# State reads of an attention stage: four matmuls of 32 by 64 on column tiles in place of one of 128 by 256

## The chip, the cores and the metric

The kernel runs on one core of a Trainium2 chip. A time is that of one execution on the device, in microseconds (us), from the first to the last instruction and what the launch puts around it. Shorter is better. The engines of the core are named as in the profile: PE is TensorE's matmuls and PEld its weight loads, DVE is VectorE, ACT is ScalarE, POOL is GpSimd, SP is the queue of SyncE, which here only issues DMAs.

## The reference

Three layers follow each other: an attention between 512 tokens and 32 state vectors for each of 8 batches and 8 heads, a top-1 mixture of experts with a capacity, and a gated feed-forward layer.

```python
B, H, S, Ns, D = (8, 8, 512, 32, 64)
scores = scale * np.matmul(x, state.transpose(0, 1, 3, 2))
a = softmax(scores); xread = np.matmul(a, state)
scores2 = scale * np.matmul(state, x.transpose(0, 1, 3, 2))
a2 = softmax(scores2)
sread = np.matmul(a2, x)                       # the state reads: 32 x 512 by 512 x 64, per batch and head
x = np.concatenate([xread, sread], axis=2)     # then gate, greedy assignment, experts, feed-forward
```

## The kernel before

The kernel is one program for one core. Its attention stage takes the batches b = 0 to 7 in turn. A string of steps for each batch (HEAD, ORDER, NEXT, LAST, TAIL, lines 53 to 57) says in which order the code is written; a scheduler under it then sets each engine's order from dependences and a cost table of its own, so a step can end up beside one of the next batch. The steps that matter here:

- z (`scores`, L302 to L304): scores of four heads at a time (g = 0, 1), state index by head on the 128 partitions (head h of the group on partitions 32h to 32h+31), the 512 tokens on the free axis.
- f (`exps2`, L324 to L326): row maximum on DVE, exponential `e2` on ACT. t (`turn_e2`, L350, L351): PE turns `e2` so that tokens lie on partitions; ACT copies the result to `et`.
- m (`center`, L310 to L314) and e (`exps1`, L335 to L338): the other softmax, DVE `zt`, POOL `zc`, DVE `zb`, ACT `e1h` and `zb`, POOL `e1l`. r (`xread`, L357 to L383): the token reads `px` from these, copied by ACT (`xu`, L374).
- s (`sread`, L414 to L439): the state reads. For each g the four token blocks r add up in `ps`. The weights are the 128 columns of `et` (four heads by 32 states), and the moving side holds the 256 columns of the four heads (4 by 64). So all 4 by 4 pairs of heads are computed and the four diagonal blocks are used. DVE then multiplies each diagonal block by `rd2` into `ss` (L433, four instructions of 32 partitions by 128), SP stores `ss` to `xm_d` in four DMAs (L438).
- G (`sread_gate`, L441 to L451): PE turns `ss` (L443), ACT copies it to `TS` (L444), and after the fourth and the eighth batch PE multiplies `TS` by the gate's weights (L449).
- p (`prep_state`, L241 to L254: ACT `SBh` L247, DVE `SBl` L252, ACT `sT` L254), q (`prep_gate`, L262 to L270: PE with 64 rows of weights, ACT `SC` and `RBh`, POOL `RBl`), x (`turn_x`, L285 to L289): operands of the next batch.

A float32 matmul of the program stands in the trace as two pairs of weight load and matmul: the 64 matmuls of L422 are 128 there. The last steps of the stage (TAIL) go over into the selection: `keys` and `count128` (L506, L517) need the gate's results of the last batch. The selection, the experts and the feed-forward layer follow; they are the other 1240 us of the program.

Of the kernel before, what the change touches and what calls it, by code (L numbers as in the profile page):

```python
# [21 lines left out]
F32 = mybir.dt.float32  # L22
# [9 lines left out]
B, H, S, D, NS = 8, 8, 512, 64, 32  # L32
# [32 lines left out]
def moe_kernel(ctx: ExitStack, tc: tile.TileContext, x, state, moe_w_gate, moe_w1, moe_w2,  # L65
               moe2_w_gate, moe2_w_val, moe2_w_out, out):
    nc = tc.nc
# [25 lines left out]
    ap = a_ctx.enter_context(tc.tile_pool(name="ap", bufs=1, space=PSUM))  # L93
# [38 lines left out]
    for q in range(2):  # L132
        pair = []
        for part in "hl":
            t = ac.tile([128, 4, 128], FR, name=f"SB{part}{q}")
# [3 lines left out]
    for q in range(3):  # L139
        pair = []  # L140
        for part in "hl":
            t = ac.tile([128, 2, 4, ROW], FR, name=f"RB{part}{q}")
# [271 lines left out]
    def sread(b, part):  # L414
        t = st[b]
        xc, et = xcs[b], t["et"]
        if part == 0:
            t["ps"] = ap.tile([128, 2, 256], F32, name="ps")
        ps = t["ps"]
        for g in (part,):  # L420
            for r in range(4):
                nc.tensor.matmul(ps[:, g, :], et[:, r, g, :],  # L422
                                 xc[:, r, 4 * g:4 * g + 4, :].rearrange("p h d -> p (h d)"),
                                 start=(r == 0), stop=(r == 3))
        if part == 0:
            return
        rd2 = aw.tile([128, 2], F32, name="rd2")
        nc.vector.tensor_scalar(rd2, t["den2"], 1e-9, None, op0=OP.add)
        nc.vector.reciprocal(rd2, rd2)
        ss = aw.tile([128, 2, D], F32, name="ss")  # L430
        for h in range(4):
            p = slice(32 * h, 32 * h + 32)
            nc.vector.tensor_mul(ss[p], ps[p, :, 64 * h:64 * h + 64],  # L433
                                 rd2[p, :, None].to_broadcast([32, 2, D]))
        r0 = b * SE + S
        for h in range(4):
            dst = xm_d[r0:r0 + NS].rearrange("n (g h d) -> n g h d", g=2, h=4)[:, :, h, :]
            nc.sync.dma_start(dst, ss[32 * h:32 * h + 32])  # L438
        t["ss"] = ss  # L439
# [266 lines left out]
    for b in range(B + 1):  # L706
        steps = {0: HEAD, B - 2: NEXT, B - 1: LAST, B: TAIL}.get(b, ORDER)
        for op in steps.split():
# [5 lines left out]
            elif k == "m" and b < B:  # L714
                center(b, q)
            elif k == "f" and b < B:
                exps2(b, q)
            elif k == "e" and b < B:
                exps1(b, q)
            elif k == "q" and b + 1 < B:  # L720
                prep_gate(b + 1)
            elif k == "R":
                read_gate(b - 1)
            elif k == "r":
                xread(b - 1, q)
            elif k == "t":
                turn_e2(b - 1, q)
            elif k == "x" and b + 1 < B:
                turn_x(b + 1, q)
            elif k == "s":  # L730
                sread(b - 1, q)
            elif k == "g":
                sread_gate(b - 1)
            elif k == "G" and b > 1:
                sread_gate(b - 2)
            elif k == "p" and b + 1 < B:
                prep_state(b + 1)
            elif k == "k":
                keys(0, PRE, True)
                part_p = ap.tile([128, 512], F32, name="pt", bufs=3)  # L740
                count128(0, PRE, part_p[:, :E])
                part = sel.tile([128, E], F32, name="part")
                nc.vector.tensor_copy(part, part_p[:, :E])
# [664 lines left out]
    for s, (gi, jj) in enumerate(outs):  # L1408
# [5 lines left out]
        if s + 1 < len(outs):  # L1414
            r, t = SETS[s % 2] if s > 1 else YR
# [82 lines left out]
```

## Time and profile before

| | us |
|---|---|
| median of 3 runs (1386.87 to 1389.83) | 1388.23 |
| the profiled execution | 1388.9 |
| its span, first to last instruction | 1387.1 |
| PE busy in the span | 1338.2 |
| PE at L422 (state reads), 128 matmuls, busy | 31.1 |
| DVE at L433 (`ss`), 32 instructions, busy | 9.1 |

Busy time of PE is the union of matmuls whose ends are modelled, and each such matmul lies over the start of the next; so what a matmul costs in a row of them is read from the start of one to the start of the next. "Idle before" is what an engine waited, with the engine that ended the wait.

### The profile page before, as it was taken

What the parts mean: (1) busy time and instruction counts of PE and PEld (TensorE: products, weight loads), DVE (VectorE), ACT (ScalarE), POOL (GpSimd) and SP (SyncE); (2) the same over time, 40 slices, a digit from 0 to 9 for tenths busy, and PEclk for the clock granted to TensorE, in tenths of its full rate; (3) what the DMA queues carried; (4) which work ended last, traced back from release to release, by engine and by line L of the source; (5) the groups of instructions that cost most, each with busy time, mean ns of one, the idle gap of its engine ahead of it and who ended that gap; (6) DMA issues with size and microseconds to landing.
All of it is one profiled execution on the core that took longest, in us unless ns stands there. A gap on an engine that the chain in (4) does not pass through costs nothing.

```text
span 1387.1 us, 27011 instructions
## 1 busy us (share of the span) xinstructions
PE 1338.2 (96%) x10176; PEld 1301.4 (94%) x10177; DVE 1068.7 (77%) x2211; ACT 572.3 (41%) x1175; POOL 440.1 (32%) x378
## 2 busy tenths in 40 slices
PE   6998599999999999999999999999999999999997
PEld 4887489999999999999999999999999999999997
DVE  6878788886887664668777787878777678888784
ACT  5886334233333343434233343434343354344342
POOL 6666111110101010343223120111111008788883
PEclk9999699999999999999999999999999999999999
DMA  7551325544445454536654676787665584444432
GB/s 138 125 128 69 135 83 183 184 157 144 160 159 161 157 176 149 188 109 245 209 199 149 216 245 207 253 259 240 219 221 174 192 279 131 144 152 143 163 108 77
DMA packets 151251, 236.89 MB, mean 171 GB/s; under 512 B 57808, under 2 KB 77264, under 8 KB 150096
## 3 DMA queue, kind: packets, MB, share of 16 engines
q1 hardware_dynamic: 138016, 208.38, 46.1%
q0 software_dynamic: 5536, 17.83, 3.9%
q10 hardware_dynamic: 7568, 8.95, 2.1%
q8 instruction: 80, 1.31, 0.4%
q14 instruction: 51, 0.42, 0.1%
HBM read 151.22 MB, written 83.89 MB: 170 GB/s over the span
## 4 chain that ended last, share of the span: by engine, by line
PE 50%; DMA 1%; DVE 1%; POOL 0%; issue 0%; POOLq 0%; SPq 0%; DVEq 0%
PE b L1157 50%; DMA mt_d<-m 1%; DMA raw<-v_d 0%; DMA v_d<-f32v 0%; POOL tt L930 0%; DVE yb L887 0%; POOL tt L929 0%; DVE m L1203 0%; POOL tt L928 0%; POOL tt L927 0%; POOLq L1493 0%; DVE u L1215 0%; DVE f32v L233 0%; DVE f32v L231 0%; DVE m L1222 0%
## 5 line engine op out<-in xcount | busy, mean ns | idle before, releaser
L1157 PE MATMUL b<-yb,w 128*128 128x364 f32 (+1 forms) x3024 | 500.5, 328 | 2.9 <-DVE m L1203 2.9
L1157 PEld LDWEIGHTS b<-yb,w 128*128 128x128 f32 x3024 | 499.5, 188 | 3.8 <-DVE m L1203 3.8
L1157 PE MATMUL b<-w,yb 128*128 128x256 f32 x2160 | 256.0, 281 | 0.0
L1157 PEld LDWEIGHTS b<-w,yb 128*128 128x128 f32 x2160 | 255.6, 189 | 0.3 <-issue 0.2
L846 PE MATMUL h<-xh,w 128*128 128x288 f32 (+1 forms) x1024 | 207.9, 295 | 1.5 <-ACT xh L830 1.2
L846 PEld LDWEIGHTS h<-xh,w 128*128 128x128 f32 x1024 | 161.6, 189 | 2.5 <-ACT xh L830 1.8
L816 POOL DMA_INDIRECT xg<-xm_d,idx x38 | 45.7, 1203 | 360.3 <-PE bt L825 155.7
L846 PE MATMUL h<-xl,w 128*128 128x288 f32 (+1 forms) x512 | 147.9, 291 | 0.0
L861 PE MATMUL y<-hh,w 128*128 128x288 f32 (+1 forms) x512 | 136.1, 292 | 0.1
L862 PE MATMUL y<-hh,w 128*128 128x288 f32 (+1 forms) x512 | 135.8, 291 | 0.0
L850 ACT ACTIVATE hh<-h 128x288 fp32r<-128x288 f32 (+1 forms) x128 | 50.8, 397 | 186.5 <-PE h L846 173.3
L1204 ACT ACTIVATE m<-m 128x364 f32<-128x364 f32 (+1 forms) x108 | 54.8, 507 | 156.0 <-DVE m L1203 147.7
L887 DVE TENSOR_TENSOR yb<-ty,yb 128x512 fp32r<-128x512 f32 (+2 forms) x96 | 87.8, 921 | 18.8 <-ACT yb L886 17.0
L861 PEld LDWEIGHTS y<-hh,w 128*128 128x128 f32 x512 | 96.6, 189 | 0.3 <-ACT hh L850 0.3
L862 PEld LDWEIGHTS y<-hh,w 128*128 128x128 f32 x512 | 96.7, 189 | 0.0
L846 PEld LDWEIGHTS h<-xl,w 128*128 128x128 f32 x512 | 96.1, 189 | 0.3 <-DVE xl L831 0.2
L914 POOL TENSOR_TENSOR tt<-raw 128x512 f32<-128x512 f32 (+1 forms) x23 | 29.6, 1290 | 208.3 <-DMA raw<-m_d 154.4
L851 DVE SCALAR_TENSOR_TENSOR hl<-h,hh 128x288 fp32r<-128x288 f32 (+1 forms) x128 | 56.0, 438 | 51.4 <-ACT hh L850 50.8
L886 ACT CAST yb<-ty 128x512 fp32r<-128x512 f32 (+2 forms) x96 | 66.5, 694 | 68.9 <-POOL ty L915 33.9
L865 PE MATMUL y<-hl,w 128*128 128x288 f32 (+1 forms) x512 | 87.9, 291 | 0.0
L887 DVE TENSOR_TENSOR yb<-yr,yb 128x512 fp32r<-128x512 f32 (+2 forms) x73 | 71.6, 982 | 6.3 <-ACT yb L886 5.5
L1207 DVE TENSOR_TENSOR m<-cv,m 128x364 f32<-128x364 f32 (+1 forms) x108 | 66.1, 612 | 9.4
(284 smaller groups left out, 2230.5 us busy)
## 6 DMA issues: line engine op xcount, KB each, us to landing
raw<-in_moe_w_dram SPq DMA_DIRECT2D x64, 512.0 KB, 4.8
raw<-m_d SPq DMA_DIRECT2D x14, 1024.0 KB, 5.6
raw<-v_d SPq DMA_DIRECT2D x26, 512.0 KB, 4.5
yr<-m_d SPq DMA_DIRECT2D x13, 1024.0 KB, 5.2
yr<-y_d SPq DMA_DIRECT2D x7, 1456.0 KB, 7.7
v_d<-f32v SPq DMA_DIRECT2D x36, 256.0 KB, 3.5
m_d<-m SPq DMA_DIRECT2D x48, 182.0 KB, 3.0
m_d<-m SPq DMA_DIRECT2D x24, 364.0 KB, 4.5
```

Of the source, the lines that this page charges most:

```text
L816: hooks["g"] = nc.gpsimd.indirect_dma_start(out=xg[:n], out_offset=None, in_=xm_d, in_offset=bass.IndirectOffsetOnAxis(ap=idx[i][:n, j:j + ...
L846: hooks["p"] = nc.tensor.matmul(ph, W[i][0][k][q == 1][:, fs], (xl if q == 2 else xh)[:, k, :T], start=(n == 0), stop=(n == 11)).ins
L850: relu[16 * i + 8 * hf + f] = hooks["hh"] = nc.scalar.activation(hh, ph, AF.Relu).ins
L851: lower[16 * i + 8 * hf + f] = hooks["h"] = nc.vector.scalar_tensor_tensor(hl, ph, 0.0, f32(hh), op0=OP.max, op1=OP.subtract).ins
L861: nc.tensor.matmul(p[d], wh[:, f % 2, ds_], hh, start=(f == 0), stop=False)
L862: nc.tensor.matmul(p[d], wl[:, f % 2, ds_], hh, start=False, stop=False)
L865: nc.tensor.matmul(p[d], wh[:, f % 2, ds_], hl, start=False, stop=(f == 7))
L886: nc.scalar.copy(hi, src)
L887: nc.vector.tensor_tensor(lo, src, f32(hi), OP.subtract)
L1157: nc.tensor.matmul(out, a, b, skip_group_check=True, start=start and n == 0, stop=stop and n == len(terms) - 1)
L1204: hooks["silu"] = nc.scalar.activation(m[:, l], m[:, l], AF.Silu).ins
L1207: hooks["gate"] = nc.vector.tensor_tensor(m[:, l], c, m[:, l], OP.mult).ins
```

## The change

Each matmul of `sread` becomes four. Head h of the group gets a matmul of its own with the 32 weight columns that belong to it, the 64 moving columns that belong to it, and the output partitions 32h to 32h+31, which puts it on column tile h of the array (all 128 rows, 32 columns). Only the diagonal blocks are computed. `ps` shrinks from 256 to 64 columns for each g, and since the blocks of the four heads then stand under each other, one multiplication of 128 partitions by 128 replaces the four of 32. Each half g of a batch has 16 matmuls in the program (32 pairs of load and matmul) where it had 4 (8 pairs); over the stage 64 become 256, and 32 instructions of DVE become 8. The four stores of `ss` stay.

```diff
-            t["ps"] = ap.tile([128, 2, 256], F32, name="ps")
+            t["ps"] = ap.tile([128, 2, D], F32, name="ps")
...
             for r in range(4):
-                nc.tensor.matmul(ps[:, g, :], et[:, r, g, :],
-                                 xc[:, r, 4 * g:4 * g + 4, :].rearrange("p h d -> p (h d)"),
-                                 start=(r == 0), stop=(r == 3))
+                for h in range(4):
+                    p = slice(32 * h, 32 * h + 32)
+                    nc.tensor.matmul(ps[p, g, :], et[:, r, g, p], xc[:, r, 4 * g + h, :],
+                                     start=(r == 0), stop=(r == 3))
...
         ss = aw.tile([128, 2, D], F32, name="ss")
-        for h in range(4):
-            p = slice(32 * h, 32 * h + 32)
-            nc.vector.tensor_mul(ss[p], ps[p, :, 64 * h:64 * h + 64],
-                                 rd2[p, :, None].to_broadcast([32, 2, D]))
+        nc.vector.tensor_mul(ss, ps, rd2[:, :, None].to_broadcast([128, 2, D]))
```

The scheduler's order changes with it, from the first state read on and up to the last matmuls of the attention stage; the order of everything behind is the same. Three places of a batch in the middle of the stage show it.

DVE, from the fourth-to-last `SBl` (low part of the next batch's state) to `zb` (the turned scores that ACT waits for), before:

```order
L252 TENSOR_TENSOR SBl_101<-pt,SBh_99 64x2x32
L380 TENSOR_TENSOR xw<-xu,rd 128x128
L382 COPY rm<-rd 128x16
L252 TENSOR_TENSOR SBl_101<-pt,SBh_99 64x2x32
L387 TENSOR_REDUCE Lw<-xw 128x32
L252 TENSOR_TENSOR SBl_101<-pt,SBh_99 64x2x32
L310 STREAM_TRANSPOSE zt<-z_611 128x512
L324 TENSOR_REDUCE mx<-z_650 128x1
L312 TENSOR_REDUCE m_667<-zt 128x16
L325 TENSOR_SCALAR nmx<-mx 128x1
L289 TENSOR_TENSOR xTl<-pt,xTh 128x4x128 x2
L310 STREAM_TRANSPOSE zt<-z_650 128x512
```

and now:

```order
L382 COPY rm<-rd 128x16
L387 TENSOR_REDUCE Lw<-xw 128x32
L310 STREAM_TRANSPOSE zt<-z_632 128x512
L252 TENSOR_TENSOR SBl_101<-pt,SBh_99 64x2x32 x4
L312 TENSOR_REDUCE m_688<-zt 128x16
L324 TENSOR_REDUCE mx<-z_671 128x1
L289 TENSOR_TENSOR xTl<-pt,xTh 128x4x128
L325 TENSOR_SCALAR nmx<-mx 128x1
L289 TENSOR_TENSOR xTl<-pt,xTh 128x4x128
L335 STREAM_TRANSPOSE zb<-zc 128x512
```

`xw`, `rm`, `Lw` and the first `zt` moved ahead of the four `SBl`, and `zb` follows the second `xTl` directly; the second `zt` comes behind it.

ACT in the same batch, from the second `zb` to the copy `TS` of the state reads, before:

```order
L337 ACTIVATE zb<-zb 128x512
L266 COPY SC<-pt 32x2x8 x4
L269 CAST RBh_103<-SC 32x2x74 x4
L374 COPY xu<-px 128x296 x2
L247 CAST SBh_95<-pt 64x2x32 x4
L351 COPY et<-pt 128x512 x2
L326 ACTIVATE e_827,den_826<-z_819,nmx 128x512
L254 COPY sT<-pt 64x256
L444 COPY TS<-pt 128x4x32
```

and now:

```order
L266 COPY SC<-pt 32x2x8 x4
L269 CAST RBh_103<-SC 32x2x74 x4
L374 COPY xu<-px 128x296
L336 ACTIVATE e1h<-zb 128x512
L374 COPY xu<-px 128x296
L337 ACTIVATE zb<-zb 128x512
L247 CAST SBh_95<-pt 64x2x32 x2
L326 ACTIVATE e_869,den_868<-z_861,nmx 128x512
L247 CAST SBh_95<-pt 64x2x32 x2
L351 COPY et<-pt 128x512 x2
L442 COPY TS<-pt 128x4x32
```

The second `e1h` and `zb` moved behind `RBh`, and `TS` follows `et` directly, where `e` and `sT` stood between the two.

PE in the one batch of the middle that has the gate's matmuls on `TS` (L449 before, L447 now), before:

```order
L443 MATMUL pt<-ident,ss 128x128
L357 MATMUL px<-RBh_107,e1h 128x296
L358 MATMUL px<-RBl_109,e1h 128x296
L359 MATMUL px<-RBh_107,e1l 128x296
L449 MATMUL pt<-wgp,TS 128x8 x4
L285 MATMUL pt<-ident,xc 128x128 x4
```

and now:

```order
L441 MATMUL pt<-ident,ss 128x128
L359 MATMUL px<-RBh_107,e1l 128x296
L357 MATMUL px<-RBh_107,e1h 128x296
L358 MATMUL px<-RBl_109,e1h 128x296
L359 MATMUL px<-RBh_107,e1l 128x296
L447 MATMUL pt<-wgp,TS 128x8 x4
L285 MATMUL pt<-ident,xc 128x128 x4
```

Four token reads stand between the turn of `ss` and the gate's matmuls, where three stood.

## Rows read from the trace of the kernel before

**Rows 1.** Window of the attention's middle: length, busy by engine (instructions), granted clock, DMA
```profile
34.03:116.56 82.53, 79.34 (x472) 68.21 (x470) 69.16 (x182) 71.21 (x203) 57.00 (x58) 0.98 0.47 119
```
**Rows 2.** Windows by batch, between first score matmuls; engines PE, PEld, DVE, ACT, POOL
```profile
70.09:84.37 14.28, 13.88 (x86) 11.80 (x85) 12.33 (x34) 12.67 (x37) 10.23 (x12) 1.00 0.64 155
84.37:102.16 17.79, 16.20 (x94) 14.03 (x92) 13.47 (x37) 13.25 (x40) 11.26 (x11) 0.90 0.51 122
```
**Rows 3.** Timeline of PE, one batch: start, length, instruction, count
```profile
75.11 0.38 PE L357 MATMUL px<-RBh,e1h 128*128 128x296 f32 x1
...
76.84 1.89 PE L422 MATMUL ps<-xc,et 128*128 128x256 f32 x8
...
78.70 0.30 PE L358 MATMUL px<-RBl,e1h 128*128 128x296 f32 x1
...
81.06 1.89 PE L422 MATMUL ps<-xc,et 128*128 128x256 f32 x8
82.88 0.63 PE L262 MATMUL pt<-wg,sT 64*128 64x32 f32 x4
83.44 0.40 PE L357 MATMUL px<-RBh,e1h 128*128 128x296 f32 x1
```
**Rows 4.** Timeline of weight loads at L262 of another batch: idle before, and its end
```profile
68.61 0.52 PEld L262 LDWEIGHTS pt<-wg,sT 64*128 64x128 f32 x4 [0.33 <-issue]
```
**Rows 5.** Line L517: lengths in ns, first and last start
```profile
L517 PE MATMUL pt<-G,I x24: 165/167/181, 138.7 to 139.3; 128*128 128x8 bf16 x24
```
**Rows 6.** Timelines of ACT and POOL in that batch: start, length, idle before
```profile
69.99 0.71 ACT L266 COPY SC<-pt 32x16 f32<-32x16 f32 x4
...
72.68 0.87 ACT L247 CAST SBh<-pt 64x64 fp32r<-64x64 f32 x4
...
74.67 0.69 ACT L326 ACTIVATE e<-z,nmx 128x512 f32<-128x512 f32 x1
...
80.44 0.63 ACT L336 ACTIVATE e1h<-zb 128x512 fp32r<-128x512 f32 x1 [0.46 <-DVE zb L335]
...
83.03 0.66 ACT L336 ACTIVATE e1h<-zb 128x512 fp32r<-128x512 f32 x1
...
84.26 0.72 ACT L266 COPY SC<-pt 32x16 f32<-32x16 f32 x4
...
84.33 1.28 POOL L338 TENSOR_TENSOR e1l<-zb,e1h 128x512 fp32r<-128x512 f32 x1
```
**Rows 7.** Timeline of DVE in that batch, and one row of the stage's end
```profile
75.66 0.23 DVE L252 TENSOR_TENSOR SBl<-pt,SBh 64x64 fp32r<-64x64 f32 x1
...
76.56 0.65 DVE L324 TENSOR_REDUCE mx<-z 128x1 f32<-128x512 f32 x1
77.25 0.69 DVE L312 TENSOR_REDUCE m<-zt 128x16 f32<-128x512 f32 x1
...
77.91 1.28 DVE L289 TENSOR_TENSOR xTl<-pt,xTh 128x512 fp32r<-128x512 f32 x2
...
79.73 0.67 DVE L335 STREAM_TRANSPOSE zb<-zc 128x512 f32<-128x512 f32 x1
...
84.05 1.22 DVE L433 TENSOR_TENSOR ss<-ps,rd 32x128 f32<-32x128 f32 x4
...
119.42 0.29 DVE L380 TENSOR_TENSOR xw<-xu,rd 128x128 f32<-128x128 f32 x1
```
**Rows 8.** PE at the gate's matmuls, and the window right behind, columns as in Rows 1
```profile
90.75 1.06 PE L449 MATMUL pt<-wgp,TS 128*128 128x8 f32 x8 [1.52 <-ACT TS L444]
91.66 0.73 PE L285 MATMUL pt<-ident,xc 128*128 128x128 f32 x4
...
92.06:95.48 3.42, 3.42 (x14) 3.06 (x12) 2.25 (x5) 2.26 (x5) 1.05 (x1) 0.50 1.08 307
```
**Rows 9.** Timelines of PE and DVE at the end of the attention stage
```profile
132.83 3.70 PE L422 MATMUL ps<-xc,et 128*128 128x256 f32 x16
...
146.69 0.17 DVE L530 TENSOR_TENSOR ev<-acc,part 128x8 f32<-128x8 f32 x1 [1.02 <-PE acc L517]
```

## The prediction

> **What bounds the kernel now.** I read the windows first, to see where the changed lines run, then the timelines of one batch engine by engine, to see who waits for whom. The state reads run in the attention stage only; its middle, 82.53 us, holds five and a half rounds of one batch each [rows 1]. No engine is alone the bound there. In a round of 14.28 us PE is busy 13.88, ACT 12.67, DVE 12.33 and POOL 10.23 [rows 2], and PE's share is flattered, because each of its matmuls is drawn over the start of the next. The reader should look for the loop that sets the 14.28. It is this: ACT begins `e1h` when DVE's `zb` is done (80.44, after 0.46 idle), works on to `SC` at 84.26 and to the end of `SBh`, which in the round before came at 73.55, 3.56 after the `SC` at 69.99 [rows 6]; DVE then goes from its first `SBl` to the end of `zb` at 80.40 [rows 7], and ACT begins again. That is 3.82 + 3.56 + 6.85, or 14.2. Neither the state reads on PE nor the products `ss` on DVE lie on this loop. So the change gains in the middle only by way of what the new order does to the loop, or loses if PE becomes longer than it.
>
> **A second loop goes over PE.** `SC` starts, ACT comes to the second `zb`, POOL makes `e1l`, PE does the token reads, both blocks of state reads and L262, and the next `SC` may start. Before, it has some slack. In the new order the second `e1h` and `zb` come behind `RBh`. From `SC` to the end of that `zb` are 3.56 less 0.87 for `SBh` plus 1.23 for the two (83.03 to 84.26), or 3.9; `e1l` adds 1.28 [rows 6]. On PE, 1.7 pass from the first token read to the first block, 2.5 between the end of that block (78.56, which is the start of L358 less the 0.14 of a token read) and the second, and 0.66 for L262 with what stands before it [rows 3]. That makes 10.1 without the two blocks.
>
> **The blocks.** Removed: 8 pairs of load and matmul at 0.215 (76.84 to 78.56) in each block, 3.44 a round [rows 3]. Added: 64 pairs a round, each with a quarter of the weight columns and a quarter of the moving columns. The trace has no column tile, so the price of a pair is bounded. One matmul of 64 columns streams a quarter of 0.215, 54 ns. The cheapest pair in the trace is 26 ns: 24 pairs with 8 moving columns start within 0.6 us [rows 5]; four tiles that work side by side can come down to it. The dearest would add a load that hides under nothing: L262 has four pairs in 0.56 with loads of 128 columns, 0.14 each [rows 3], 27 ns for 32 columns in proportion, so 81 ns a pair; 0.19 if a load of 32 columns costs as much as one of 128. I take 40 ns. The two pairs of one float32 matmul go to the same tile, so each second pair must wait 54 ns for its own tile, and each other one needs the 26 of the cheapest row; it is nearest to the row of L517. The block's own loads before hide wholly under the running matmul, since 0.215 is the streaming time alone.
>
> The trace does show what another shape of weights costs. Before L262, with 64 rows, the weight load has 0.33 idle that no engine ended [rows 4]. The block's last matmul stops streaming at 82.78, and L262 starts at 82.88 [rows 3], 0.1 later, and its first load is not hidden. I take 0.12 to enter a block (0.1 and a load of 27 ns) and 0.2 to leave it (0.1 and a load of 128 columns). The second block already runs into L262, so only three of the four passages are new: 0.44 a round.
>
> At 40 ns PE's loop is thus 10.1 + 2.6 + 0.4, or 13.1. At 26 ns it is 12.2, at 54 ns 14.0, at 81 ns 15.7.
>
> [...]
>
> **ACT and DVE in the new order.** ACT's part from `e1h` to the end of `SBh`: 3.82 + 3.56 as before, and `e`, 0.69, which now stands between the `SBh`: 8.1 [rows 6]. DVE's part is now four `SBl` (0.9), `m` 0.69, `mx` 0.65, `xTl` 1.28 and `zb` 0.67, 4.2 [rows 7]; `xw`, `Lw` and both `zt` moved out of it. With 0.3 for the small steps and hand-overs this loop is 12.6, which is ACT's whole work in a round [rows 2]. The products `ss` fall from 1.22 to the 0.29 of the nearest product of 128 by 128 [rows 7], 0.9 less on DVE, whose sum becomes 11.4; that alone ends nothing sooner. If it cost nothing less, DVE would still fit. So PE's 13.1 is late next. The real round is longer than its longest loop, as engines meet on buffers, and I take 13.3: **1.0 less a round**, 5.0 over five rounds (no gain counted in the half one).
>
> **The gate's matmuls.** One round takes 17.79 [rows 2]. [...] In the new order ACT copies `TS` directly behind `et`, not behind `e` and `sT`, and PE has one token read more to do first. The excess of 3.51 less the 0.9 that stays is 2.6; I take 2.3, and 1.5 if the clock falls all the same.
>
> **The end.** In the last batch PE works on 16 matmuls of state reads from 132.83 on, 3.4 at 0.215, and at the end DVE waits 1.02 for PE [rows 9]. 64 pairs at 40 ns and the passages save 0.6 there; four products less in `ss` save 0.9, of which part waits behind PE's queue. I take 1.2 less for both. The stores of `ss` stay four on SP, and each now waits for the one product, which is over sooner than the fourth was; SP's other DMAs, the loads of `xc`, keep their distance.
>
> Behind the attention stage the order is the same and starts sooner by as much. **Sum** against the profiled execution's 1388.9: less 5.0, 2.3 and 1.2, which is 8.5: 1380.4. That execution is 0.7 above the median of the runs, so their spread adds no more than that.
>
> **The rivals.** *One tile after the other.* The array streams the four tiles in turn and hides the loads: 54 ns a pair, PE's loop 14.0, only 0.3 less a round. With 2.3 at the gate and 0.5 at the end that is 4.3 less, 1384.6. The change would then not do what it says. For it: every row of the trace shows one matmul after the other; against it: no row has two tiles.
>
> *Loads in the open.* The pair costs 81 ns: PE's loop of 15.7 becomes the bound of every round, 1.4 more each, 7.0; the end costs 1.3 more and the gate gains 1.5, so 6.8 more: 1395.7, slower. From 58 ns a pair PE's loop is longer than today's round; from about 66 ns the total is a loss. Against it: the loads of L422 hide today; for it: those of L262 don't at its start. At 0.19 the kernel would be at some 1430, to which I give next to nothing.
> [...]
>
> *A slower clock.* PE has less to stream and idles more; if the clock falls once a round as at 92.06, each fall costs the 1.1 that remain of the 3.51 beside the wait and L449. Five and the one at the gate take 6.6 of the 8.5: 1387.0. For it: the fall followed 1.5 of idle time; against it: the rounds beside it have 0.4 idle and a clock of 1.00 [rows 2].
>
> **How the numbers follow.** About 0.2% (2.8 us) is what a measurement of this kernel can tell from no change. My forecast has 0.50: 0.45 faster, 0.03 within, 0.02 slower, as the new order can also lose. One tile after the other 0.20: 0.13, 0.05, 0.02. Loads in the open 0.18: 0, 0.02, 0.16. Slower clock 0.12: 0.04, 0.05, 0.03. Together faster 0.62, within 0.15, slower 0.23. The range 1374 to 1391 goes from a pair of 26 ns with rounds near ACT's 12.7 (1.6 less each, 5.0 + 3.0 + 3.5) to the slower clock and one tile after the other with the order losing some; it leaves out most of the loads in the open and little below, under 0.2.
>
> **What would show it.** Right: blocks of 32 pairs in 1.2 to 1.4 us on PE, rounds of 13 to 13.5, no wait for `TS` over 0.3, a clock of 1.00 up to the stage's end, `ss` in one instruction of about 0.3. Wrong: blocks of 1.8 (one tile after the other) or over 2.5 (loads in the open), rounds of 14 or more, falls of the clock inside rounds, or a round set by POOL, which has no part in the sum.

## The result

| | before | after |
|---|---|---|
| median, us | 1388.49 (1386.87 to 1389.83) | 1375.22 (1374.47 to 1376.23) |
| the profiled execution | 1388.9 | 1376.23 |
| its span | 1387.1 | 1374.5 |

After to before is 0.9905, 95% interval [0.9888, 0.9923]: faster by 13.3 us, where 8.5 was forecast. The span is 12.5 shorter (1387.05 and 1374.53 before rounding). In the lines below, line numbers of after are those of before less 2 from `ss` on, and 2 more in `sread`'s matmul: L424 (before L422), L432 (L433), L441 (L443), L447 (L449).

A round below goes from a batch's first score matmul to the next batch's; the gate's round is the one that holds the gate's matmuls on `TS`, and the three full rounds ahead of it are called plain. The windows by batch of the kernel after, with columns as in [rows 2] (length, busy time of PE, PEld, DVE, ACT, POOL with counts, granted clock, DMA share and rate): a plain round, the gate's round and the last round.

```profile
65.74:78.61 12.87, 11.79 (x131) 10.01 (x131) 12.08 (x31) 12.24 (x37) 10.26 (x11) 1.00 0.74 170
78.61:92.54 13.93, 12.94 (x139) 11.00 (x139) 12.35 (x32) 12.53 (x37) 10.29 (x11) 1.00 0.75 172
92.54:107.19 14.65, 12.76 (x136) 10.45 (x135) 12.55 (x31) 14.09 (x45) 12.94 (x16) 1.00 0.35 107
```

A plain round takes 12.87 where it took 14.28, the gate's 13.93 where it took 17.79 [rows 2], both at a clock of 1.00. PE's busy time in a plain round is 2.1 shorter. ACT, with 12.24 of 12.87, is now the fullest engine, with DVE right behind it. The only wait of ACT that the view of this plain round names is short:

```profile
ACT e L326 <- DVE nmx L325: 0.3, 1, 0.3
```

So the round is now little more than ACT's own work.

The timeline of PE after, over the first block of a round, its waits in the next round, and at the gate's matmuls. The first three rows are the same block, cut off after one, four and eight pairs:

```profile
61.03 0.24 PE L424 MATMUL ps<-xc,et 128*32 128x64 f32 x1
61.03 0.26 PE L424 MATMUL ps<-xc,et 128*32 128x64 f32 x4
61.03 0.32 PE L424 MATMUL ps<-xc,et 128*32 128x64 f32 x8
61.03 0.65 PE L424 MATMUL ps<-xc,et 128*32 128x64 f32 x32
61.61 0.41 PE L357 MATMUL px<-RBh,e1h 128*128 128x296 f32 x1
...
67.89 0.50 PE L303 MATMUL z<-xTl,SBh 128*128 128x512 f32 x1 [0.72 <-DVE xTl L289]
...
72.24 0.33 PE L441 MATMUL pt<-ident,ss 128*128 128x128 f32 x1 [0.26 <-ACT et L351]
...
85.70 0.31 PE L359 MATMUL px<-RBh,e1l 128*128 128x296 f32 x1
85.85 1.02 PE L447 MATMUL pt<-wgp,TS 128*128 128x8 f32 x8
```

Four pairs start within 0.02 us (0.26 less the 0.24 that the first is drawn). The next four come 0.08 later, and each further four 0.056 after those before. The trace does not name the tile of a pair; with 54 ns of streaming a pair [rows 3], four starts every 56 ns read as one on each column tile. The 32 pairs start within 0.43 (0.65 less the 0.22 that a later one is drawn), 14 ns a pair, and the next instruction starts 0.58 after the block's start; a block took 1.72 before [rows 3]. PE now waits 0.72 for DVE's `xTl` and 0.26 for ACT's `et` in a round, and not at all for `TS`.

Timelines of POOL and DVE after, in a plain round and at the stage's end:

```profile
65.88 1.34 POOL L338 TENSOR_TENSOR e1l<-zb,e1h 128x512 fp32r<-128x512 f32 x1
...
65.99 1.26 DVE L382 COPY rm<-rd 128x16 f32<-128x16 f32 x1
...
67.76 0.27 DVE L432 TENSOR_TENSOR ss<-ps,rd 128x128 f32<-128x128 f32 x1
...
70.81 0.16 DVE L382 COPY rm<-rd 128x16 f32<-128x16 f32 x1
...
118.73 1.96 POOL L383 TENSOR_TENSOR xm<-xu,rm 128x1024 f32<-128x1024 f32 x1 [2.23 <-ACT zb L337]
...
118.91 1.81 DVE L478 TENSOR_TENSOR key<-V,sg 128x24 int32<-128x24 int32 x1
...
134.85 0.17 DVE L528 TENSOR_TENSOR ev<-acc,part 128x8 f32<-128x8 f32 x1 [0.17 <-PE acc L515]
```

`ss` is one product of 0.27. The last row stood at 146.69 before [rows 9], so the attention stage gives 11.84 of the span's 12.5. One copy `rm`, 128 by 16, takes 0.16, and another of the same size 1.26, beside an `e1l` of POOL that began 0.1 before it; `key`, a small operation too, takes 1.81 and ends with an `xm`. The prediction has no term for these rows.

In the five rounds of the stage's middle the clock is 1.00, but not up to the stage's end. Windows there, before and then after:

```profile
139.00:147.00 8.00, 7.65 (x64) 7.47 (x61) 4.91 (x27) 4.69 (x24) 0.00 (x0) 0.57 0.29 110
```

```profile
124.00:135.00 11.00, 10.81 (x122) 10.45 (x123) 7.53 (x35) 5.00 (x25) 1.91 (x1) 0.53 0.27 104
```

In the last stretch of the stage the granted clock of the changed kernel is at 0.50 for some 10 us (a mean of 0.53 over these 11.00) where that of the kernel before was for some 7 (0.57 over 8.00). Ahead of the first full round it is the other way round: a mean clock of 0.81 over 18.12 us before, 0.89 over 16.03 after.

### The profile page after: what moved, and what is told of

Read it like the earlier page. It is cut to its first block, busy times and chain, and to the rows that moved or that the text cites. A ratio compares the mean times of both kernels' runs of the same rounds, so it can differ in the third digit from the quotient of the medians.

```text
span 1374.5 us, 27733 instructions
## 1 busy us (share of the span) xinstructions
PE 1322.4 (96%) x10560; PEld 1286.9 (94%) x10561; DVE 1067.5 (78%) x2187; ACT 568.9 (41%) x1175; POOL 439.7 (32%) x378
## 4 chain that ended last, share of the span: by engine, by line
PE 51%; DMA 1%; DVE 1%; issue 0%; ACT 0%; POOLq 0%; DVEq 0%; SPq 0%
PE b L1155 51%; DMA yr<-m_d 1%; ACT yb L884 0%; DVE m L1201 0%; DVE yb L885 0%; DVE m L1205 0%; ACT m L1202 0%; DMA mt_d<-m 0%; DVE u L1213 0%; POOLq L1491 0%; DVE w L885 0%; ACT w L884 0%; DVE cv L1204 0%; DVE m L1220 0%; DVEq L1201 0%
## 5 line engine op out<-in xcount | busy, mean ns | idle before, releaser
L885 DVE TENSOR_TENSOR yb<-ty,yb 128x512 fp32r<-128x512 f32 (+2 forms) x96 | 88.0, 924 | 18.2 <-ACT yb L884 17.1
L1205 DVE TENSOR_TENSOR m<-cv,m 128x364 f32<-128x364 f32 (+1 forms) x108 | 69.1, 640 | 10.2 <-ACT m L1202 1.1
```

Source lines behind the costliest of these rows:

```text
L885: nc.vector.tensor_tensor(lo, src, f32(hi), OP.subtract)
L1205: hooks["gate"] = nc.vector.tensor_tensor(m[:, l], c, m[:, l], OP.mult).ins
```

## The experiments

**How the order was separated from the instructions.** The scheduler gave the changed kernel another order, so the change is three things at once: blocks, products and order. In most of the kernels below every instruction of the attention stage is chained behind the one that goes ahead of it on its engine, in an order read off one of the two kernels ("old order", "new order"). This fixes the issue order and is meant to add no wait. No run chains the kernel after, as it is, in its own order; that the chain costs little shows in no_copy_before and filled, whose times are those of before and after. The edit at its core:

```diff
+    for engine, text in QUEUES.items():          # the order, step by step
+        last = None
+        for word in text.split():
+            name, _, n = word.partition("*")
+            for _ in range(int(n or 1)):
+                i = todo[engine, name].pop(0)
+                if last is not None:
+                    tc.add_manual_dep(i, last.name, NoSync, reason="pin")
+                last = i
```

The times of all runs, each with its ratio to runs of before on the same chip. "Plain rounds" gives the second and third of the five full ones, the gate's round is the fourth, each from first score matmul to first score matmul. one_tile_in_turn and after are not chained; the order of one_tile_in_turn in the full rounds came out nearly as that of after:

| kernel | order | blocks | products | copy `rm` | plain rounds | gate's round | median | ratio, 95% interval |
|---|---|---|---|---|---|---|---|---|
| before | old | old | four | yes | 14.3 | 17.8 | 1388.5 | 1 |
| blocks_old_order | old | new | four | yes | 14.3 | 15.4 | 1383.77 | 0.9970 [0.9959, 0.9982] |
| new_in_old_order | old | new | one | yes | 14.3, 14.6 | 15.2 | 1383.16 | 0.9968 [0.9957, 0.9979] |
| ts_first | old, `TS` moved | old | four | yes | 14.3 | 14.6 | 1384.98 | 0.9976 [0.9966, 0.9985] |
| old_in_new_order | new | old | four | yes | 14.4, 14.6 | 17.1 | 1391.13 | 1.0025 [1.0015, 1.0034] |
| no_copy_old_in_new | new | old | four | no | 14.4 | 15.3 | 1388.70 | 1.0007 [0.9997, 1.0016] |
| four_products | new | new | four | yes | 14.5 | 15.0 | 1385.20 | 0.9985 [0.9975, 0.9994] |
| no_copy_four_products | new | new | four | no | 12.4, 12.7 | 13.9 | 1378.93 | 0.9937 [0.9920, 0.9955] |
| one_tile_in_turn | new | new, a tile at a time | one | yes | 13.8 | 15.0 | 1384.47 | 0.9977 [0.9967, 0.9987] |
| after | new | new | one | yes | 12.9 | 13.9 | 1375.22 | 0.9905 [0.9888, 0.9923] |
| no_copy | new | new | one | no | 12.4, 12.7 | 15.4 | 1377.62 | 0.9927 [0.9909, 0.9945] |
| own_bank_no_copy | new | new | one | no | 12.7 | 15.3 | 1378.17 | 0.9932 [0.9909, 0.9956] |
| filled | new | new | one | no | 12.7 | 13.9 | 1375.48 | 0.9904 [0.9887, 0.9921] |
| no_copy_before | old | old | four | no | 14.0 | 15.9 | 1388.62 | 1.0006 [0.9997, 1.0016] |

**Is it the order or the shorter work? New instructions in the old order, and the reverse.** The edit is the chain alone.

> The changed instructions (column-tile blocks, one product ss) with every engine's order of the attention stage pinned to that of the kernel before. Theory 'order': the shorter blocks and products lie off the loop that sets the round (ACT e1h to SBh, DVE SBl to zb), so the rounds stay at 14.2 us, PE still waits over 1 us for TS, since ACT still does e and sT first, and only the stage's end gains: 1385.5 to 1387.5. Theory 'shorter blocks': the 1.2 us that each of two blocks and the 0.9 that the products lost go straight into the round: rounds of 13.0 to 13.4, total 1375 to 1380, as in the changed kernel.

> The instructions of before (128 by 256 matmuls, four products of 32 partitions) with every engine's order of the attention stage pinned to that of the changed kernel. Theory 'order': the round is the longer of the ACT and DVE loop in the new order (12.6 forecast, 12.9 seen) and PE's loop with old blocks, 10.1 + 3.44 = 13.5; so rounds of 13.5, the gate's wait for TS gone (2.3), total 1381 to 1384, half of the gain or more. Theory 'shorter blocks': rounds of 14.2 or more, total 1387 to 1392.

Windows of one plain round, first of new_in_old_order, with a wait of PE at the end of the round ahead of it and one in the gate's round:

```profile
69.85:84.46 14.61, 13.30 (x133) 11.46 (x132) 11.48 (x32) 12.86 (x37) 10.53 (x11) 0.86 0.68 155
```

```profile
68.93 0.40 PE L422 MATMUL px<-RBh,e1h 128*128 128x296 f32 x1 [1.46 <-ACT xu L439]
...
91.16 1.06 PE L512 MATMUL pt<-wgp,TS 128*128 128x8 f32 x8 [0.87 <-ACT TS L507]
```

and of old_in_new_order:

```profile
70.60:85.21 14.61, 13.46 (x85) 11.86 (x84) 14.10 (x34) 12.40 (x36) 10.44 (x11) 1.00 0.61 149
```

Neither half does it alone. The new instructions in the old order leave the rounds at 14.3 to 14.6, as "order" expected: what PE saves comes back as a wait for ACT's `xu` (the 14.6 has a fall of the granted clock in it, 0.86 in the mean). The gain of 4.6 us (0.32%), more than that theory gave, lies outside the plain rounds. The new order with the old instructions loses 3.4 us (0.25%), as "shorter blocks" expected and far over the range of "order". So each theory fails in one of the two runs. In old_in_new_order DVE is busy 14.10 of 14.61, 1.8 more than before [rows 2]. The next runs ask where DVE's time comes from.

**The blocks alone, in the old order.** blocks_old_order keeps the four products:

```diff
-        nc.vector.tensor_mul(ss, ps, rd2[:, :, None].to_broadcast([128, 2, D]))
+        for h in range(4):
+            p = slice(32 * h, 32 * h + 32)
+            nc.vector.tensor_mul(ss[p], ps[p], rd2[p, :, None].to_broadcast([32, 2, D]))
```

> The column-tile blocks alone, with the four products of before, in the order of before. Blocks and one product in the old order took 4.6 off (1383.2). If the products end nothing sooner in the old order, where no copy rm is held, this kernel has the same time, 1383 to 1384; if they are worth their 0.9 in some rounds or at the end, 1385 to 1388.

The window of a plain round of it:

```profile
68.95:83.26 14.31, 12.07 (x133) 9.85 (x132) 12.34 (x34) 12.47 (x37) 10.23 (x11) 1.00 0.67 153
```

1383.77, the same within the intervals as with one product (1383.16). In the old order the products end nothing sooner, as the prediction said, and blocks that are 2.3 shorter a round on PE leave the round at 14.31.

**The products in the new order.** four_products has the same edit, chained in the new order.

> The changed kernel, order pinned, but with four products ss of 32 partitions by 128 in place of one: DVE has 0.9 us more a batch. If DVE's sum only has to fit into the round (11.4 + 0.9 of 12.9), rounds stay at 12.9 and only the end gives back 0.5 to 0.9: 1375.5 to 1377. If ss lies on the chain that sets the new round, each of five rounds gives back 0.9 and the total is 1380 to 1381.

The window of a plain round, the line of all its copies `rm` (shortest, median, longest in ns), and DVE's and POOL's timeline where one of them is held:

```profile
67.14:81.62 14.48, 11.96 (x131) 10.00 (x132) 13.97 (x34) 12.25 (x37) 10.32 (x11) 1.00 0.59 157
```

```profile
L450 DVE COPY rm<-rd x14: 159/1244/1259, 39.4 to 132.6; 128x16 f32<-128x16 f32 x14
```

```profile
72.77 1.28 POOL L406 TENSOR_TENSOR e1l<-zb,e1h 128x512 fp32r<-128x512 f32 x1
...
72.84 1.24 DVE L450 COPY rm<-rd 128x16 f32<-128x16 f32 x1
```

1385.20: in the new order the products are worth some 10 us, not 0.9 a batch. DVE is busy 13.97 where it is 12.08 after, so 1.9 more. The products are 0.9 of it; the other 1.0 or so is the second copy `rm`, which now begins 0.07 after an `e1l` and lasts 1.24, to 0.03 after its end. Expected was 0.9 a round at most; it was 1.6.

In these rows the long instruction of DVE begins just behind one of POOL and ends with it: the copy takes 1.24 in place of 0.16, and `key` at 118.91 above, which began 0.18 after an `xm`, took 1.81 where it takes 0.18 in the kernel before, and ended 0.03 after that `xm`. "Held" stands here for such an instruction. That POOL's instruction is what holds it is the author's reading of these times; no run shows by what means. Who begins first made the difference in these traces: the copy at 45.08 in the kernel after begins 0.01 ahead of an `e1l` and takes 0.16, and so does the second copy of a round in one_tile_in_turn (below):

```profile
73.25 0.16 DVE L382 COPY rm<-rd 128x16 f32<-128x16 f32 x1
...
73.26 1.30 POOL L338 TENSOR_TENSOR e1l<-zb,e1h 128x512 fp32r<-128x512 f32 x1
```

**Without the copy.** POOL's `xm` reads `rd` itself, in each of four kernels:

```diff
-            rm = aw.tile([128, 2, H], F32, name="rm", bufs=2)
-            nc.vector.tensor_copy(rm, rd)
-            nc.gpsimd.tensor_tensor(xm[:, q], xu[:, :, :, :D], rm[:, :, :, None].to_broadcast([128, 2, H, D]), OP.mult)
+            nc.gpsimd.tensor_tensor(xm[:, q], xu[:, :, :, :D], rd[:, :, :, None].to_broadcast([128, 2, H, D]), OP.mult)
```

> The new blocks with four products ss of 32 partitions, in the new order, without the copy rm. With the copy its rounds were 14.5, 1.6 over the changed kernel's, and both copies of a round took 1.25. Theory 'held copy': of the 1.6 the products themselves are 0.9 and the second held copy the rest; without copies DVE's sum is 13.98 less 2.5, or 11.5, and rounds fall to 12.4 to 13.2, total 1374 to 1379. Theory 'the products alone': rounds stay over 14, total 1383 to 1386.

> The instructions of before in the new order, without the copy rm, of which both in each round took 1.25 us. Theory 'held copy': what kept the new order from gaining by itself was DVE; without the copies PE's loop with old blocks, 10.1 + 3.44 = 13.5, is what is left: rounds of 13.3 to 13.8 in place of 14.4, total 1384 to 1387. Theory 'blocks': PE's longer blocks alone held it at 14.4, total 1390 to 1392.

> The kernel before in its own order, without the copy rm, of which 13 of 14 took 0.17 us or less there. Theory 'held copy': nothing to gain, as no copy in its rounds is held: 1387 to 1388.5. If the copy costs in another way (POOL reading later, a semaphore), it gains here too: below 1386.

> The changed kernel, order pinned, without DVE's copy rm of 128 by 16: POOL's xm reads rd itself. In the changed kernel one copy a round takes 1.25 us where it takes 0.16 elsewhere, and ends 0.03 after POOL's e1l that began 0.1 before it. Theory 'held copy': that copy holds DVE up on the chain that sets the round, 12.9; without it the round falls towards ACT's whole work of 12.3: rounds of 12.3 to 12.5, total 1370 to 1373. Theory 'DVE has slack there': rounds stay at 12.9, total 1374.5 to 1376.

Windows of a plain round of no_copy_four_products:

```profile
53.55:65.92 12.37, 11.42 (x132) 9.94 (x131) 11.24 (x31) 11.96 (x36) 9.51 (x10) 1.00 0.52 135
```

of no_copy_old_in_new, and PE's wait in the next round:

```profile
55.98:70.39 14.41, 13.48 (x84) 11.89 (x83) 12.13 (x32) 12.61 (x36) 10.26 (x11) 1.00 0.62 151
```

```profile
76.57 0.33 PE L508 MATMUL pt<-ident,ss 128*128 128x128 f32 x1 [0.94 <-ACT et L418]
```

and three rounds of no_copy, with PE's waits in them:

```profile
38.91:53.27 14.36, 12.06 (x128) 10.24 (x126) 13.55 (x31) 12.03 (x34) 10.40 (x11) 0.88 0.56 141
53.27:65.68 12.41, 11.41 (x133) 9.95 (x132) 10.46 (x28) 12.00 (x36) 9.64 (x10) 1.00 0.57 142
78.40:93.77 15.37, 14.12 (x140) 12.06 (x140) 11.96 (x31) 12.75 (x38) 10.70 (x12) 0.89 0.81 180
```

```profile
45.68 0.33 PE L506 MATMUL pt<-ident,ss 128*128 128x128 f32 x1 [2.30 <-ACT et L418]
...
72.17 0.33 PE L506 MATMUL pt<-ident,ss 128*128 128x128 f32 x1 [1.24 <-ACT et L418]
...
84.90 0.33 PE L506 MATMUL pt<-ident,ss 128*128 128x128 f32 x1 [1.25 <-ACT et L418]
```

With four products the copy explains most of the loss: plain rounds fall from 14.5 to 12.4 and 12.7, the total from 1385.20 to 1378.93, the far end of what "held copy" expected. So four products cost little once no copy is held, 1.3 us beside no_copy, with intervals that overlap. With the old blocks it does not: DVE's 14.10 becomes 12.13, but the round stays at 14.4, as PE's 13.48 and its wait of 0.94 for `et` fill it. "Held copy" was wrong there; it had left that wait out of PE's loop. Its total, 1388.70, lies between the two ranges. The kernel before gains nothing in total from the same edit (1388.62), as expected: its plain rounds are 0.3 shorter, about the time of two copies of 0.16, and the gate's 1.9, but the last round is 1.5 and the end 0.9 longer.

no_copy missed both expectations. The copy did hold the round, which falls to 12.41 where nothing else interferes. But the total is no lower, 1377.62 (0.9927 beside 0.9905 after, intervals that overlap). PE, with DVE out of its way sooner, waits 1.00 to 2.30 for ACT's `et` ahead of the turn of `ss`. Some 0.4 and 2.2 us behind two of these waits the granted clock falls to half (0.52 and 0.51 in the means below), and those rounds take 14.36 and 15.37. Windows of no_copy at these falls:

```profile
46.00:49.50 3.50, 3.50 (x45) 2.87 (x44) 2.92 (x7) 2.85 (x9) 2.33 (x2) 0.52 0.44 178
87.00:90.50 3.50, 3.50 (x42) 2.77 (x41) 2.30 (x5) 1.85 (x4) 1.03 (x2) 0.51 0.82 246
```

A wait of the same 1.24, at 72.17, was followed by no fall. four_products had longer waits for the same buffer, one in each of four rounds (in all, times, longest), at a clock of 1.00 throughout:

```profile
PE pt L511 <- ACT et L419: 6.2, 4, 2.2
```

So a wait of this length alone does not bring the fall.

**Is it the wait that brings the fall?** Two kernels without the copy, both with `ps` widened to 512 columns: in own_bank_no_copy PE turns `ss` into unused columns of it, in place of a buffer that `et` must free; in filled PE multiplies the identity by itself during the wait (four matmuls a round, nine in the first; their result is not used).

```diff
-        pt = ap.tile([128, 512], F32, name="pt", bufs=3)
-        nc.tensor.transpose(pt[:, :128], st[b]["ss"].rearrange("p g d -> p (g d)"), ident)
+        ps = st[b]["ps"]
+        nc.tensor.transpose(ps[:, 128:256], st[b]["ss"].rearrange("p g d -> p (g d)"), ident)
```

```diff
+        for _ in range(9 if b == 0 else 4 if b < 5 else 0):
+            nc.tensor.matmul(st[b]["ps"][:, 128:256], ident, ident, start=True, stop=True)
         pt = ap.tile([128, 512], F32, name="pt", bufs=3)
```

> The kernel without the copy rm, and with PE's turn of ss written into the unused columns of the state reads' own PSUM bank, where it took one of the three shared buffers pt, the one that ACT's et frees: without the copy PE waits there for et, 1.24 us in a round and 2.30 in the first, and the granted clock was 0.5 for 3.5 us behind two of these waits (rounds of 14.4 and 15.4 beside 12.4 and 12.7). Theory 'the wait brings the fall': the wait for et is gone, the clock stays at 1.00 in the rounds, all are 12.3 to 12.7: total 1371 to 1374.5, below the changed kernel. Theory 'PE idles anyway': the idle time moves to another place, the clock falls there, total 1376 to 1379.

> The changed kernel without the copy rm (as no_copy, order pinned), and with matmuls of the identity by itself (128 by 128, result unused) on PE ahead of the turn of ss, where PE waits for et: four in a round, some 0.8 us of the 1.24 us wait, and nine in the first round, where it waits 2.30. Without the copy two rounds were 12.4 and 12.7, but in two others the granted clock fell to 0.5 for 3.5 us behind this wait, and they took 14.4 and 15.4. Theory 'idle PE, then the fall': with the wait filled the clock stays at 1.00 in the rounds, which take 12.3 to 12.8 (the gate's round 13.3 to 13.9): total 1371 to 1374.5, below the changed kernel. Rival 'falls come elsewhere' or 'the filling delays the turn': rounds of 12.9 and more, or a fall in one of them, total 1375 to 1379.

Windows of a plain round and the gate's round, first of own_bank_no_copy, with a wait of PE in the latter:

```profile
65.98:78.67 12.69, 11.68 (x131) 9.96 (x131) 11.08 (x29) 12.09 (x37) 10.18 (x11) 1.00 0.76 174
78.67:94.00 15.33, 14.26 (x139) 12.11 (x139) 11.98 (x31) 12.65 (x38) 10.70 (x12) 0.89 0.81 181
```

```profile
85.50 0.40 PE L426 MATMUL px<-RBh,e1l 128*128 128x296 f32 x1 [1.07 <-POOL e1l L405]
```

then of filled:

```profile
53.51:66.18 12.67, 12.31 (x139) 10.89 (x139) 11.06 (x29) 12.23 (x37) 10.15 (x11) 1.00 0.72 165
78.90:92.82 13.92, 13.56 (x147) 11.88 (x147) 11.37 (x30) 12.49 (x37) 10.21 (x11) 1.00 0.76 176
```

In own_bank_no_copy the idle time moved: PE waits 1.07 for `e1l` in the gate's round, the clock falls there (0.89 in the mean) and the total is 1378.17, as the rival expected. A wait of 1.67 for `et` in its first full round stays, on another instruction, with no fall behind it. In filled the clock stays at 1.00 in all rounds, and the gate's round is back at 13.92. Busy PE, no fall: this fits the theory, in one trace, but does not show it, as waits of this length elsewhere had no fall behind them either. The total, 1375.48, misses its range: it is that of the changed kernel, not below. With the copy gone and the clock up, a round is 12.7, ACT's 12.23 of work and little else, so the held copy costs the changed kernel some 0.2 a round at most (the 12.41 of no_copy follows a round with a fall). No version beat it. At the stage's end the edit even has a price, in the timelines of POOL and DVE of no_copy:

```profile
108.72 1.92 POOL L448 TENSOR_TENSOR xm<-xu,rd 128x1024 f32<-128x1024 f32 x1
...
108.87 1.92 DVE L447 TENSOR_TENSOR xw<-xu,rd 128x128 f32<-128x128 f32 x1
```

Without the copy `xm` needs only `rd`, as `xw` does, and begins 0.15 ahead of it; `xw` then lasts 1.92, where it takes 0.28 in three of the changed kernel's last four and 1.05 in the other. The long time is not gone but stands on another instruction; what that costs in total was not separated.

**What a pair costs when its tile is busy.** one_tile_in_turn swaps the loops:

```diff
-            for r in range(4):
-                for h in range(4):
-                    p = slice(32 * h, 32 * h + 32)
+            for h in range(4):
+                p = slice(32 * h, 32 * h + 32)
+                for r in range(4):
```

> The changed kernel with the loops over heads and token blocks swapped: the eight pairs of one head stand in a row, so one column tile takes eight pairs before the next tile begins. It prices what the prediction took for every second pair. 'One after the other': a pair costs the 54 ns of its stream, a block of 32 is 1.75 us where the changed kernel has 0.45, PE's loop is 10.1 + 3.5 + 0.4 = 14.0, rounds of about 14, total 1380 to 1384. 'Loads in the open': a load waits for the running matmul of its own tile, 81 ns or more a pair, blocks of 2.6, rounds of 15 or more, total over 1388. 'No matter which tile': 14 ns again, blocks under 0.6, total 1375.

PE's timeline, the first row cut off after five pairs, then the block, with the wait ahead of it; and the window of that round:

```profile
75.09 0.33 PE L441 MATMUL pt<-ident,ss 128*128 128x128 f32 x1 [0.94 <-ACT et L351]
...
76.78 0.47 PE L424 MATMUL ps<-xc,et 128*32 128x64 f32 x5
...
76.78 1.39 PE L424 MATMUL ps<-xc,et 128*32 128x64 f32 x32
78.10 0.40 PE L357 MATMUL px<-RBh,e1h 128*128 128x296 f32 x1
```

```profile
68.89:82.71 13.82, 12.88 (x133) 11.44 (x132) 12.32 (x31) 12.62 (x36) 10.30 (x11) 1.00 0.61 159
```

The first five pairs, all on one tile, start within 0.25 (0.47 less 0.22), 62 ns a pair. Over the block it is 38 ns (1.39 less 0.22, by 31): neither of the first two cases nor the third, but between. The single starts in the trace tell why. They fall into four rows of eight, 80 ns and then 56 ns apart, 0.415 us from a row's first start to its last, and each row begins 0.25 after the one before, while that has three pairs to go. The starts of the changed kernel's block fall into the same four rows of 0.415, but all four begin within 0.02. Read as the four tiles, this says that a tile takes its eight pairs at one pace in both kernels, and only the order decides how many tiles work at a time.

Rounds of 13.8 are near what "one after the other" expected, and 1384.47 is just above its range, but not for its reason. With 1.17 a block PE's loop as the prediction sums it is 10.1 + 2.3 + 0.4, or 12.8; the rest is the wait of 0.94 for `et`, which is in this kernel's rounds as in those of no_copy_old_in_new. So PE's length matters in the new order: blocks longer by 0.74 each make the round longer by 0.9.

**The step at the gate by itself.** ts_first is the kernel before, chained in its own order, with one instruction of ACT moved:

```diff
-5.t1 5.f0 5.p 5.G
+5.t1 5.G 5.f0 5.p
```

> The kernel before, every engine's order pinned, with one step moved: in the batch of the gate's matmuls ACT's copy TS comes directly behind et, ahead of e and sT, as in the changed kernel. The prediction gave this step 2.3 of the 8.5. If it holds: no wait for TS over 0.3, no fall of the clock there, the round 15.2 to 15.6 in place of 17.8, total 1385 to 1386.5. Rival 'the wait is only part': PE waits for something else at the same place or the clock falls at another, the total stays within 1 us of before, 1387 to 1388.5.

The window of the gate's round, and PE at the gate's matmuls:

```profile
84.61:99.21 14.60, 14.54 (x94) 12.70 (x92) 12.60 (x35) 12.98 (x39) 10.50 (x11) 1.00 0.61 147
```

```profile
89.40 1.06 PE L514 MATMUL pt<-wgp,TS 128*128 128x8 f32 x8
```

No wait, no fall, a round of 14.60 in place of 17.79, and 3.2 us less in total (0.24%), a little more than expected: one copy earlier on ACT is worth a quarter of what the whole change gave.

## Why the prediction was right, and where it was off

| term | forecast | measured in the two traces |
|---|---|---|
| half round ahead of the full ones | 0 | -1.50 (first score matmul at 40.08, was 41.58) |
| three plain rounds | -1.0 each | -1.47, -1.38, -1.40 |
| gate's round | -1.0 and -2.3 | -3.87 |
| last round | -1.0 | +0.25 |
| the end, to `ev` | -1.2 | -2.47 |
| behind the stage | 0 | -0.68 |
| sum | -8.5 | -12.52, the span's difference |

- **The sum and its range.** Of the 4.0 that the sum misses, the five rounds hold 0.6 (7.3 forecast with the gate, 7.9 measured), as three plain rounds and the gate gained more and the last round nothing. The other 3.4 came from the half round, the end and the part behind the stage. The lower end of the range is not what the prediction derives for it: 1388.9 less 11.5 is 1377.4, and the result lies below that, in the slack down to 1374. That it lies inside the range is luck in part. Of the signs named for "right", the missing wait for `TS` and the short `ss` came; blocks (0.43 to 0.58) and rounds (12.9) came out shorter than named, and the clock did not stay at 1.00 up to the stage's end.
- **The loops were right.** Neither the blocks nor the products lie on the loop of before: new_in_old_order and blocks_old_order have the old rounds. The gain of a round comes through the new order, and only with the shorter work in it. With the old instructions in the same order DVE is busy 14.10 (old_in_new_order), and once the copies are gone PE's 13.48 and its wait of 0.94 still fill 14.4 (no_copy_old_in_new).
- **The price of a pair was mis-sized**: 40 ns taken, 14 measured, below the lower bound of 26. The step that failed is "each second pair must wait 54 ns for its own tile". The wait itself exists (56 to 80 ns a pair in one_tile_in_turn), but by the starts the pairs of the other tiles do not queue behind it. So the 26 from [rows 5], where every pair takes all 128 columns of the array, was no lower bound for four tiles. PE's loop by the prediction's sum becomes 10.1 + 0.9 + 0.4, or 11.4, and not PE but ACT, with the loop forecast at 12.6, is late next; the round measures 12.9. That is the 0.4 a plain round that was missing. The 27 ns of a load in the open is a smaller slip: a quarter of the row's 0.14 is 35, so that rival's pair is 89 by the row, not 81.
- **Loads in the open** did not come: four pairs of load and matmul start every 56 ns, where one pair's stream alone is 54 by the estimate from [rows 3], and that leaves no room for a load in the open, though each of these matmuls uses all 128 rows (128*32 in the timeline). The starts of one_tile_in_turn go further: a row of eight, read as one tile's, begins while three pairs of the row ahead still wait. The prediction did not weigh that.
- **`ss`** fell to 0.27 as forecast. "If it cost nothing less, DVE would still fit" failed in the new order: four_products loses 10 us. The sum of DVE's work, 11.4 and 0.9, left out the held copies, up to 2.2 a round (two, at 1.25 for 0.16). The trace of before shows one such copy of 1.24 at 39.5, outside the rows that were read.
- **The gate's step** was right in mechanism and about in size: 2.3 forecast. The 0.9 taken to stay is L449's time, and the fall is the clock of 0.50 behind PE's wait of 1.52 [rows 8]. The excess of the gate's round over a plain one fell from 3.51 to 1.06, so 2.45; ts_first alone gives 3.2.
- **The end and the half round** were too small. In the half round the clock differs from kernel to kernel: blocks_old_order, with -1.6 there, had 1.00 in the window where before had 0.81, and new_in_old_order, with -0.7, had 0.80. At a like clock the shorter work is thus worth about 0.7 in that one pair of traces; how much of the -1.5 the clock gave is not separated. The end gained 2.5 although the clock was down for longer there; what gave it was not tested. The last round gained nothing: ACT is busy 14.09 of 14.65 there. Of the 0.7 behind the stage no cause was tested.
- **The rivals.** "One tile after the other" was priced at a round of 14.0 and 1384.6; when the loops force something near it, the runs give 13.8 and 1384.47, in part by PE's wait for `et`, which the rival did not have, so the agreement is luck in part. "A slower clock" did not come in the changed kernel's five rounds, only at the stage's end; it did come in rounds of no_copy and own_bank_no_copy, where a fall costs some 1.5 (15.37 beside filled's 13.92 in the gate's round, 14.36 beside filled's 12.75 in the first), not 1.1.

## What to carry to other kernels

A part that shortens work off the binding loop pays only if the order lets another loop shrink with it; pin the order and swap the instructions to see which of the two it is, since each alone may give nothing or a loss. Small matmuls that went round four tiles cost 14 ns a pair here, and 38 with each tile's eight pairs in a row, so try the loop over tiles inside. When an engine's sum "would still fit", look first whether a few of its short instructions take many times their usual length (1.25 for 0.16 us here), and beside whose work.

## What the runs showed of the hardware

- Pairs of load and matmul of 32 columns by 64 moving columns start 14 ns apart in the order of the changed kernel (32 starts within 0.43 us), and 38 ns apart in that of one_tile_in_turn (within 1.17). Read as tiles, the starts of one tile are 56 ns apart (80 from its first to its second), and its eight pairs take 0.415 us from first to last start in either kernel.
- A copy of 128 by 16 on DVE takes 0.16 us, and 1.24 to 1.26 when it begins 0.07 to 0.11 us after POOL's `e1l` (before at 39.49, four_products at 72.84, the kernel after once a round). When it begins 0.01 ahead of it, it takes 0.16 (the kernel after at 45.08, one_tile_in_turn at 73.25). Taking it away moved four_products by 6.3 us. Without it a product of DVE lasted 1.92 beside an `xm` of POOL (no_copy at 108.87).
- Each of the nine falls of the granted clock inside a full round, to 0.5 for some 3.4 us, came within 2.2 us behind a wait of PE of 1.0 to 2.3 us (1.07 in own_bank_no_copy, 1.25 and 2.30 in no_copy). Other such waits had no fall behind them: 1.24 in no_copy, 2.03 in the kernel after at 46.59, up to 2.2 in four rounds of four_products. What decides between them was not found.
